# A linear-attention and gated feed-forward kernel: the cosine's table loaded by its own instruction, ten warm-ups instead of twelve, and the first block's sums with two slots per matmul

## The chip, the cores and the metric

The kernel runs on one core of one Trainium2 chip. The metric is the device time of one execution in microseconds; shorter is better. Several executions are timed and the median is given. One further execution is recorded by the hardware profiler, and every row quoted here comes from such a record.

## The reference

The reference has two parts. The first is a gated linear attention over `q`, `k`, `v` and `alpha`, each of 4 batches, 8 heads, 768 time steps and 48 features, all float32:

```python
for t in range(S):
    state = alpha[:, :, t, :, None] * state + einsum('bhd,bhe->bhde', k[:, :, t], v[:, :, t])
    y[:, :, t] = einsum('bhd,bhde->bhe', q[:, :, t], state)
```

Its output, laid out as 3072 tokens of 384 features, goes through a feed-forward layer with a hidden width of 2048:

```python
h = x @ w_in
g = h * np.cos(h)
return g @ w_out
```

The result is 3072 x 384 in float32.

## The kernel before

**Tiling.** Time is cut into 24 chunks of 128 steps (6 for each batch), and four chunks make a block (`R = 4`), so there are 6 blocks. Inside a chunk the recurrence is turned into matrix products: `alpha` goes through a logarithm, running sums of the logarithms are made by matmuls with triangular masks, their exponentials scale `q` and `k`, and then scores, masked scores, outputs and the chunk's state update are ordinary matmuls. The feed-forward layer works on pairs of chunks in four quarters of the hidden width: `ff1` fills a PSUM tile, `act` makes the cosine of it on ScalarE, `gate` multiplies the two on VectorE, and `ff2` accumulates the second product.

**Order.** Nothing is scheduled automatically. A long string, `ORDER`, names units one after the other, and every engine runs its share in that order. A word such as `w12` means `warmup(12)`; `ca1` means `cums0(1)`. The suffixes `:A`, `:D` and `:P` put a unit on ScalarE, VectorE or GpSimd. All loads and stores are issued by SyncE in the same order. The string begins

```python
"a1 la1 v1 a0 la0 k1 w12 ca1 xi1 xc1 ka1 w1 ca0 q1 qa1 xi0 ct0 xt0 xc0 k0 ka0 tk1 q0 w1 tq1 w2 kp0 v0 "
```

**The first block.** Blocks 0, 1 and 2 are halved by heads, so `n = 2 * block + half`. For block 0: `a1` loads half of `alpha` (four heads), `la1` (`ln0`, L267) takes its logarithm into `lna`, whose second index is the slot `i` of 4. `ca1` (`cums0`, L281) makes, for each slot, the sum over all four slots, each multiplied by the mask `t_incl` or `t_strict`: 16 matmuls of 192 columns. `xi1` and `xc1` (`exp0`, L310) are exponentials of that sum with both signs, `ka1` and `qa1` (`hat0`, L316) multiply them into `k` and `q`. `ca0` and its followers do the same for the other half. Then `tk` and `tq` (`pe_transposes`, L373) turn the results, `kp` and `kn` (`k_rows` and `ev_k_rows`) bring `k` back to rows of time, and `S`, `u`, `A`, `m`, `Y`, `y` are the state product, its update, the scores, the mask, the outputs and their copy. Blocks 1 and 2 are in `PFX`: GpSimd forms the running sum over the slots first (`pa`, L287), and `cums0` then needs only seven matmuls for a half.

**Warm-ups.** `warmup(n)` issues `n` matmuls of 512 columns on zeros into a PSUM bank that nobody reads (L520). Twelve of them stand ahead of `ca1` in TensorE's order, and single ones stand between later units.

**Tables.** `lnset` loads the table that holds logarithm and exponential by an instruction of its own when another table is in (L179). `act` only notes that its own table is in; the load of the cosine's table (the activation function is a sine with a bias of half pi) is put in by the compiler ahead of the first `activation` that needs it, and is then recorded under that line (L483). The program has twelve table loads: six of each kind.

**Feed-forward around a table load.** With `F` for `ff1` (L477), `f` for `act` (L483), `p` for `gate` (L489), `V` for `ff2` (L497), `Z` and `z` for loads of the two weights and `R...`, `r...` for their casts, a quarter is `F`, `f`, `p` and later two `V`. The six places where `f` follows a logarithm or an exponential on ScalarE are the six loads of the cosine's table.

Of the kernel before, what the change touches and what calls it, by code (L numbers as in the profile page):

```python
# [16 lines left out]
def kernel(  # L17
# [10 lines left out]
    nc = tc.nc  # L28
    B, H, S, D = q.shape
    DM, DF = moe_w_in.shape  # L30
    C = 128
# [4 lines left out]
    R = 4  # L36
    M = C // R
    HH = H // 2
# [6 lines left out]
    PFX = (1, 2,)  # L45
# [22 lines left out]
    lna = first[:, 0 : R * H * 64].rearrange("p (i h d) -> p i h d", i=R, h=H)  # L68
    nc.gpsimd.memset(lna[:, :, :, D:64], 0.0)

    sel_f, sel_bf, t_incl, t_strict = [], [], [], []
# [32 lines left out]
    w1 = consts.tile([C, 3, DF], BF, tag="w1")  # L104
    w2 = consts.tile([C, DF // C, DM], BF, tag="w2")
# [69 lines left out]
    table = [None]  # L175
# [81 lines left out]
    HW = HH * D  # L257
# [4 lines left out]
    def hs(n):  # L262
        return slice(HH * (n % 2), HH * (n % 2 + 1))
# [6 lines left out]
    def cums0(n):  # L270
        t = ps.tile([C, 2, 512], FP, tag="big", bufs=3)
        cum0[n] = t
        lay = min(n // 2, 1)
        for i in range(R):

            if n // 2 in PFX:
                terms = [(R - 1, t_incl[lay])] if i == R - 1 else [(R - 1, t_strict[lay]), (i, ident_bf)]
            else:
                terms = [(i2, t_incl[lay] if i2 <= i else t_strict[lay]) for i2 in range(R)]
            for x, (i2, mk) in enumerate(terms):  # L280
                nc.tensor.matmul(t[:, i // 2, HW * (i % 2) : HW * (i % 2 + 1)], mk, lna[:, i2, hs(n), 0:D],  # L281
                                 start=(x == 0), stop=(x == len(terms) - 1))


    def prefix0(n):
# [192 lines left out]
                                 start=(kk == 0), stop=(kk == 2))  # L478

    def act(g, qt):  # L480
        table[0] = "sin"
        c_sb = moe.tile([C, FQ, 2, C], BF, tag="c_sb", bufs=3)
        nc.scalar.activation(out=c_sb, in_=h_ps[g, qt], func=AF.Sin, bias=halfpi, scale=1.0)  # L483
        c_t[g, qt] = c_sb
# [30 lines left out]
    def warmup(n):  # L515
# [8 lines left out]
        "a": lambda j: load("a", alpha, j), "k": lambda j: load("k", k, j),  # L524
        "q": lambda j: load("q", q, j), "v": load_v, "vn": cast_v,
        "la": ln0, "ca": cums0, "pa": prefix0, "ct": totals0, "xt": exp_tot0,
        "xi": lambda n: exp0("i", n, -1.0), "xc": lambda n: exp0("c", n, 1.0),
        "ka": lambda n: hat0("k", KO, "i", n), "qa": lambda n: hat0("q", 0, "c", n),
# [14 lines left out]
        "D": x_transposes, "B": ev_x, "X": x_transposes_dma,  # L543
        "F": lambda n: ff1(n // 4, n % 4), "Fa": lambda n: ff1(n // 4, n % 4, slice(0, 1)), "Fb": lambda n: ff1(n // 4, n % 4, slice(1, 2)),
        "f": lambda n: act(n // 4, n % 4), "p": lambda n: gate(n // 4, n % 4),
        "V": lambda n: ff2(n // 4, n % 4), "e": ev_ff2, "o": store, "w": warmup,
    }

    ORDER = (
# [64 lines left out]
```

## Time and profile before

| | us |
|---|---|
| median of 3 timed runs | 186.07 |
| lowest and highest of them | 185.19, 187.74 |
| the profiled execution | 184.71 |
| its span in the profile | 182.9 |
| TensorE busy in it (matmuls) | 174.8 |
| VectorE, ScalarE, GpSimd busy | 137.8, 115.6, 88.7 |

The span runs from the first instruction of the program to its last; the profiled execution has 1.8 us outside it. Times inside the span are counted from its start. A row of the timeline gives the start, the duration, the engine, the line of the kernel, the operation and how many instructions of this kind followed each other; brackets give the idle time of the engine before the row and what ended it. Matmuls overlap each other, so the duration of one matmul is longer than the distance from its start to the next one's start; where a rate is wanted, that distance is taken.

### The profile page before, as it was taken

The page shows a single profiled execution, that of the slowest core. Times are in us where ns is not written, and L with a number is a line of the kernel's source. Part 1 is how long each engine was busy: PE and PEld are TensorE (multiplying, and loading weights), DVE is VectorE, ACT ScalarE, POOL GpSimd, SP SyncE. Part 2 cuts the span into 40 slices and gives each one's busy share as a digit, 9 for nine tenths or more (in the row PEclk, how much of TensorE's full clock was granted, in tenths as well). Part 3 has the DMA queues.
Part 4 walks back from the last instruction along what each step waited for, and adds up shares of the span by engine and source line. Part 5 has one row for each costly group of instructions (what it writes and reads, how often), then busy time and mean ns, then how long its engine had stood idle before and what let it go on. Part 6 is the DMA issues. An engine that isn't in the chain of part 4 may idle for free.

```text
span 182.9 us, 4471 instructions
## 1 busy us (share of the span) xinstructions
PE 174.8 (96%) x1828; PEld 128.3 (70%) x1828; DVE 137.8 (75%) x178; ACT 115.6 (63%) x154; POOL 88.7 (48%) x84
## 2 busy tenths in 40 slices
PE   7999879999999999999999999999999999999992
PEld 2765668867767777777767688677767876778750
DVE  7599787989856989789569896977867859447521
ACT  3599796586849888747969766455355365474330
POOL 8004936379294999999989965931010000000000
PEclk9999999999999999999999999999999999999999
DMA  5999999998999899999689799974988304111022
GB/s 144 327 306 353 379 350 372 319 261 215 289 255 274 239 264 266 274 292 274 155 233 240 206 215 275 204 178 130 170 200 221 86 0 134 28 59 46 0 86 86
DMA packets 71524, 38.43 MB, mean 210 GB/s; under 512 B 44112, under 2 KB 68432, under 8 KB 71504
## 3 DMA queue, kind: packets, MB, share of 16 engines
q1 hardware_dynamic: 71504, 38.15, 78.3%
q8 instruction: 14, 0.23, 0.5%
q14 instruction: 6, 0.05, 0.1%
HBM read 25.17 MB, written 4.72 MB: 163 GB/s over the span
## 4 chain that ended last, share of the span: by engine, by line
PE 80%; DMA 8%; DVE 5%; ACT 2%; SPq 2%; issue 1%; DVEq 0%; ACTq 0%
PE o_new L497 32%; PE t_new L477 27%; DMA t_new<-in_moe_w_out_dram 5%; PE w_new L520 4%; PE t L392 4%; PE t L281 3%; PE t_new L373 3%; PE t L437 2%; PE t L434 2%; PE t L413 2%; DMA t_new<-in_alpha_dram 2%; DVE t L398 1%; SPq L125 1%; DMA t_new<-pre 1%; DVE pre L316 1%
## 5 line engine op out<-in xcount | busy, mean ns | idle before, releaser
L497 PE MATMUL o_new<-w,g_new 128*128 128x384 bf16 x384 | 75.8, 326 | 0.8 <-ACT o_new L164 0.4
L483 ACT ACTIVATE c_sb<-t_new,halfpi 128x1024 bf16<-128x1024 f32 x48 | 53.2, 1113 | 31.6 <-PE t_new L477 29.6
L489 DVE TENSOR_TENSOR g_new<-t_new,c_sb 128x1024 bf16<-128x1024 f32 x48 | 57.8, 1218 | 19.1 <-ACT c_sb L483 19.0
L477 PE MATMUL t_new<-x_new,w 128*128 128x256 bf16 (+1 forms) x624 | 70.9, 264 | 1.3 <-DVE w L166 0.9
L477 PEld LDWEIGHTS <-w 128*128 128x128 bf16 x624 | 56.4, 98 | 11.1 <-DVE w L166 1.2
L497 PEld LDWEIGHTS <-g_new 128*128 128x128 bf16 x384 | 34.0, 97 | 18.7 <-DVE g_new L489 1.4
L398 DVE TENSOR_TENSOR t<-t,triu_f 128x1024 bf16<-128x1024 f32 x24 | 29.0, 1217 | 2.5 <-PE t L392 2.5
L164 ACT ACTIVATE o_new<-o_new 128x384 f32<-128x384 f32 x17 | 8.3, 487 | 10.6 <-PE o_new L497 10.6
L421 DVE TENSOR_TENSOR ub<-t,em 128x384 bf16<-128x384 f32 x20 | 11.1, 557 | 2.4 <-PE t L413 1.3
L166 POOL CAST vn<-t_new 128x384 bf16<-128x384 f32 x7 | 3.5, 505 | 19.3 <-DMA t_new<-in_v_dram 19.3
L166 POOL CAST w<-t_new 128x1536 bf16<-128x1536 f32 x6 | 8.8, 1466 | 7.5 <-DMA t_new<-in_moe_w_out_dram 5.2
L316 POOL TENSOR_TENSOR pre<-t_new 128x768 bf16<-128x768 f32 x5 | 9.9, 1977 | 4.0 <-DMA t_new<-in_alpha_dram 2.2
L164 ACT ACTIVATE y_new<-t 128x384 bf16<-128x384 f32 x16 | 7.8, 489 | 5.6 <-PE t L437 5.6
L437 PE MATMUL t<-vn,t 128*128 128x48 bf16 x192 | 11.3, 184 | 0.0
L520 PE MATMUL w_new<-lnb 128*128 128x512 bf16 x26 | 9.8, 497 | 1.2 <-DVE lnb L60 1.2
L244 POOL TENSOR_TENSOR pre<-t_new,icp 128x768 bf16<-128x768 f32 x6 | 10.9, 1816 | 0.2
L437 PEld LDWEIGHTS <-t 128*128 128x128 bf16 x192 | 9.7, 96 | 1.7 <-DVE ub L421 0.5
L244 POOL TENSOR_TENSOR pre<-t_new,cp 128x768 bf16<-128x768 f32 x6 | 10.9, 1814 | 0.1
L310 ACT ACTIVATE t_new<-t 128x768 f32<-128x768 f32 x12 | 9.3, 811 | 2.0 <-PE t L281 1.8
L420 DVE TENSOR_TENSOR t<-t,ub 128x384 f32<-128x384 f32 x16 | 8.9, 559 | 1.5 <-PE t L413 1.3
L287 POOL TENSOR_TENSOR first<-first 128x192 bf16<-128x192 bf16 x12 | 7.1, 596 | 5.8 <-ACT first L267 5.1
L483 ACT ACT_TABLE_LOAD x6 | 7.7, 1283 | 3.3 <-PE t_new L477 3.3
(79 smaller groups left out, 202.4 us busy)
## 6 DMA issues: line engine op xcount, KB each, us to landing
t_new<-in_v_dram SPq DMA_DIRECT2D x24, 192.0 KB, 4.0
out_dram<-o_new SPq DMA_DIRECT2D x11, 384.0 KB, 2.8
t_new<-in_alpha_dram SPq DMA_DIRECT2D x20, 192.0 KB, 4.0
t_new<-in_k_dram SPq DMA_DIRECT2D x20, 192.0 KB, 4.3
t_new<-in_q_dram SPq DMA_DIRECT2D x20, 192.0 KB, 3.9
t_new<-in_moe_w_in_dram SPq DMA_DIRECT2D x4, 768.0 KB, 9.2
t_new<-in_moe_w_out_dram SPq DMA_DIRECT2D x4, 768.0 KB, 9.7
t_new<-pre SPq DMA_DIRECT2D x12, 256.0 KB, 3.8
```

What stands on the lines that cost most here:

```text
L164: eng.activation(out=dst, in_=src, func=AF.Copy)
L166: eng.tensor_copy(out=dst, in_=src)
L244: el(nm, b).tensor_tensor(out=pre[:, b % 2, s, off : off + 64 * H].rearrange("p i (h d) -> p i h d", d=64)[:, :, :, 0:D], in0=blk_t[nm, b] ...
L316: pick(nc.vector).tensor_tensor(out=pre[:, b % 2, :, off + 64 * HH * (n % 2) : off + 64 * HH * (n % 2 + 1)].rearrange("p i (h d) -> p i h ...
L398: nc.vector.tensor_tensor(out=t.rearrange("s (h t) -> s h t", h=H), in0=A_ps.pop(j).rearrange("s (h t) -> s h t", h=H), in1=triu_f.unsquee ...
L421: nc.vector.tensor_tensor(out=ub[:, us(j)].rearrange("r p (a e) -> r p a e", a=2), in0=t.rearrange("r p (a e) -> r p a e", a=2), in1=em_t[ ...
L437: nc.tensor.matmul(t[:, h * D : (h + 1) * D], A_t[j][:, ACOL[h] * C : (ACOL[h] + 1) * C], vn_t[j][:, h], start=first, stop=True, skip_grou ...
L477: nc.tensor.matmul(t[:, f, js], w1[:, kk, ft * C : (ft + 1) * C], x_t[g][:, js, kk], start=(kk == 0), stop=(kk == 2))
L483: nc.scalar.activation(out=c_sb, in_=h_ps[g, qt], func=AF.Sin, bias=halfpi, scale=1.0)
L489: nc.vector.tensor_tensor(out=g_new, in0=h_ps.pop((g, qt)), in1=c_t.pop((g, qt)), op=ALU.mult)
L497: nc.tensor.matmul(o_ps[j][:, 0:DM], g[:, f, j % 2], w2[:, qt * FQ + f], start=(f == 0 and qt == 0), stop=(f == FQ - 1 and qt == 3))
L520: nc.tensor.matmul(w_t[0], warm[:, 0:C], warm, start=True, stop=True)
```

## The change

There are three edits, and nothing else is changed.

1. `act` issues the load of the cosine's table by an instruction of its own, just ahead of the activation in ScalarE's order, when another table is in. The number of table loads, and the place of each among ScalarE's instructions, stay the same; the semaphore wait that stood at the load, where there was one, now stands at the activation.
2. `w12` becomes `w10`.
3. In `cums0`, block 0 takes the slots two at a time: where two neighbouring slots of the result use the same mask for a given source slot, one matmul of 384 columns reads the source slot twice through a stride of zero and writes both. Where they need different masks, two matmuls of 192 columns remain. There are 10 matmuls for a half in place of 16, six of 384 columns and four of 192; the columns add up to 3072 as before. The source slot is now the outer loop.

```diff
         lay = min(n // 2, 1)
-        for i in range(R):
-
-            if n // 2 in PFX:
+
+        if n // 2 in PFX:
+            for i in range(R):
                 terms = [(R - 1, t_incl[lay])] if i == R - 1 else [(R - 1, t_strict[lay]), (i, ident_bf)]
-            else:
-                terms = [(i2, t_incl[lay] if i2 <= i else t_strict[lay]) for i2 in range(R)]
...
+            return
+
+        for i2 in range(R):
+            for a in range(2):
+                x = lna[:, i2, hs(n), 0:D]
+                if i2 in (2 * a, 2 * a + 1) and i2 % 2 == 1:
+                    for i, mk in ((2 * a, t_strict[lay]), (2 * a + 1, t_incl[lay])):
+                        nc.tensor.matmul(t[:, a, HW * (i % 2) : HW * (i % 2 + 1)], mk, x,
+                                         start=False, stop=(i2 == R - 1), skip_group_check=True)
+                else:
+                    nc.tensor.matmul(t[:, a, 0 : 2 * HW].rearrange("p (b f) -> p b f", b=2),
+                                     t_incl[lay] if i2 <= 2 * a else t_strict[lay],
+                                     lna[:, i2 : i2 + 1, hs(n), 0:D].rearrange("p o h d -> p o h d").to_broadcast([C, 2, HH, D]),
+                                     start=(i2 == 0), stop=(i2 == R - 1), skip_group_check=True)
...
     def act(g, qt):
-        table[0] = "sin"
+        if table[0] != "sin":
+            nc.scalar.preload_act_table_set("trig_and_small")
+            table[0] = "sin"
...
-        "a1 la1 v1 a0 la0 k1 w12 ca1 xi1 ...
+        "a1 la1 v1 a0 la0 k1 w10 ca1 xi1 ...
```

More of the change, by code (lines that the diff above doesn't have):

```diff
@@ L273, in cums0 @@
         lay = min(n // 2, 1)
-        for i in range(R):
-            if n // 2 in PFX:
+        if n // 2 in PFX:
+            for i in range(R):
                 terms = [(R - 1, t_incl[lay])] if i == R - 1 else [(R - 1, t_strict[lay]), (i, ident_bf)]
-            else:
-                terms = [(i2, t_incl[lay] if i2 <= i else t_strict[lay]) for i2 in range(R)]
-            for x, (i2, mk) in enumerate(terms):
-                nc.tensor.matmul(t[:, i // 2, HW * (i % 2) : HW * (i % 2 + 1)], mk, lna[:, i2, hs(n), 0:D],
-                                 start=(x == 0), stop=(x == len(terms) - 1))
+                for x, (i2, mk) in enumerate(terms):
+                    nc.tensor.matmul(t[:, i // 2, HW * (i % 2) : HW * (i % 2 + 1)], mk, lna[:, i2, hs(n), 0:D],
+                                     start=(x == 0), stop=(x == len(terms) - 1))
+            return
[11 more added lines that the diff above has]
+                                     start=(i2 == 0), stop=(i2 == R - 1), skip_group_check=True)
     def prefix0(n):
```

2 rows, old and new, of the table ORDER are left out of this document.

## The prediction

> **What bounds the kernel now.** I read the page first: busy times and slices, then the chain that ended last.
>
> ```profile
> PE 174.8 (96%) x1828; PEld 128.3 (70%) x1828; DVE 137.8 (75%) x178; ACT 115.6 (63%) x154; POOL 88.7 (48%) x84
> PE   7999879999999999999999999999999999999992
> DMA  5999999998999899999689799974988304111022
> PE 80%; DMA 8%; DVE 5%; ACT 2%; SPq 2%; issue 1%; DVEq 0%; ACTq 0%
> ```
>
> TensorE is busy 174.8 of 182.9 us and is 80% of the chain; the DMA engines are full over the first third. So a gain must either cut TensorE work at the start or close one of its gaps. The list of waits by engine says where these are:
>
> ```profile
> PE w_new L520 <- DVE lnb L60: 1.2, 1, 1.2
> PE t_new L477 <- DVE w L166: 0.9, 1, 0.9
> PE t L281 <- DVE t L398: 0.8, 1, 0.8
> PE t_new L477 <- DVE x_new L166: 0.5, 1, 0.5
> PE o_new L497 <- ACT o_new L164: 0.4, 1, 0.4
> PE o_new L497 <- DVE g_new L489: 0.3, 1, 0.3
> PE t_new L373 <- DVE pre L316: 0.2, 1, 0.2
> ```
>
> Seven waits (total, times, longest), 4.3 us with the 1.2 us before the first warm-up; another 3.6 us at the end follow the last matmul. The windows of the later stages show that after 60 us nothing is left to close (columns: stretch, length, then each engine's busy time):
>
> ```profile
> 50.00:60.00 10.00, 9.67 (x105) 7.24 (x101) 6.10 (x9) 7.24 (x10) 6.41 (x6) 1.00 0.95 265
> 60.00:80.00 20.00, 19.95 (x228) 15.32 (x227) 17.62 (x23) 14.58 (x21) 19.69 (x13) 1.00 0.94 266
> ```
>
> So what is gained before 60 us is kept if TensorE's work then simply starts sooner. The timeline of the stages that the change touches, TensorE and then ScalarE:
>
> ```profile
> 1.19 5.30 PE L520 MATMUL w_new<-lnb 128*128 128x512 bf16 x12 [1.19 <-DVE lnb L60]
> 6.28 1.69 PE L281 MATMUL t<-first 128*128 128x192 bf16 x16
> 7.81 0.38 PE L520 MATMUL w_new<-lnb 128*128 128x512 bf16 x1
> 8.03 1.48 PE L281 MATMUL t<-first 128*128 128x192 bf16 x16
> ```
>
> ```profile
> 4.40 0.84 ACT L267 ACTIVATE first<-t_new 128x768 bf16<-128x768 f32 x1 [2.38 <-DMA t_new<-in_alpha_dram]
> 6.46 0.84 ACT L267 ACTIVATE first<-t_new 128x768 bf16<-128x768 f32 x1 [1.21 <-DMA t_new<-in_alpha_dram]
> 8.01 2.35 ACT L310 ACTIVATE t_new<-t 128x768 f32<-128x768 f32 x3 [0.71 <-PE t L281]
> 54.70 1.28 ACT L483 ACT_TABLE_LOAD   x1 [2.18 <-PE t_new L477]
> 56.00 1.11 ACT L483 ACTIVATE c_sb<-t_new,halfpi 128x1024 bf16<-128x1024 f32 x1
> 69.25 1.28 ACT L483 ACT_TABLE_LOAD   x1 [1.07 <-PE t_new L477]
> ```
>
> The logarithm that `ca1` needs ends at 4.40 + 0.84 = 5.24, but TensorE reaches `ca1` only at 6.28, behind the twelve warm-ups; ScalarE waits for it until 8.01. Two of the six loads of the cosine's table wait for a matmul before they begin.
>
> **The change part by part: ten warm-ups.** The last warm-ups start 0.427 us apart, a 512-column matmul later 0.216 us apart (7.81 to 8.03): TensorE is at half speed here, though the page's clock row shows nothing of it. The trace's clock record begins at 6.70, inside `ca1`: its first two matmuls start 0.160 us apart, the later ones 0.0825. Two warm-ups less put `ca1` at 6.28 - 0.853 = 5.43, 0.19 after its logarithm. But if the clock still rises at 6.70, 1.27 us of `ca1` now run at half speed instead of 0.42: 8 of its 16 pieces of 192 columns take 1.27, the other 8 take 0.66, and it hands over at 7.36 instead of 7.81. I take 0.45 us, not 0.85. The bounds are 0.85 (the clock rises after `ca1`) and a loss, which is the first rival.
>
> The Trainium skill, page "TensorE: Matmul & The Clock Gate", section "What's actually happening", has the full clock granted after a busy window of about 3.4 us whose phase is free of the program. By it the rise at 6.70 would stay where it is when two warm-ups go, as I assume; but in other executions it would lie elsewhere, and the gain would vary, by my estimate from that page, between about 0.2 and 0.85.
>
> **Two slots per matmul.** 32 matmuls become 20, with the same 6144 columns. The nearest row of 384 columns is `ff2`'s L497: four in 0.65 us, 0.1625 each, against 2 x 0.0825 = 0.165 for two of 192. Twelve pairs give 0.03 us. Twelve weight loads go too, but they lie beside matmuls (L281's loads take 0.098 each on PEld, with no gap between the matmuls). No row shows a moving operand with a stride of zero. Lower bound of its price: nothing. Upper bound: the source counts twice, 0.1625 more for each of twelve, 1.95 us. I take nothing, since L281 already reads 48 of every 64 elements at the rate of the contiguous L497 (0.43 and 0.42 ns a column). The new order of the terms costs nothing: the exponential reads all four slots at once.
>
> **The table.** The same twelve loads of 1.283 us remain. Where the load already follows its predecessor at once (23.40, 87.69, 98.11, 105.94) nothing changes. The one at 54.70 can start at 52.52, when ScalarE became free, and is over at 53.80, before its matmuls end at 54.6; the cosine starts at 54.7 instead of 56.0, its gate at 55.9 instead of 57.15. TensorE waited for that gate only the 0.33 us of the list (58.10 to 58.43), so of 1.3 us on ScalarE 0.33 counts. If GpSimd, busy 19.69 of the 20 us that follow, is late next with the scaled `q` and `k` of blocks 2 and 3, even that goes: bounds 0 and 0.33. The load at 69.25 starts 1.07 earlier, in a stretch in which TensorE idles 0.05: I count 0.
>
> The Trainium skill, page "ScalarE: Activation LUTs", section "What ACT_TABLE_LOAD costs", adds some 1.38 us of draining to the 1.283. The rows do not show it: the cosine follows the load by 1.30 us. By the page the gain at 54.70 would be up to 2.18 us on ScalarE, and on TensorE still 0.33.
>
> **Does the 0.45 arrive?** Following it: the exponentials start at 7.56 (their engine is free at 7.30), VectorE's first product at 8.40 instead of 8.85 (its `k` landed at 7.61). The fourth product needs the `q` that landed at 11.28, so it moves only from 11.52 to 11.30. VectorE's next gap, 0.195 us at 14.68 behind the first state product, gives most of that back: that product comes 0.45 sooner, VectorE 0.41. From there to 21.0 VectorE has no gap over 0.04, so `ca3`, which waits for its mask, moves by 0.4. The next TensorE waits (26.75, 30.98, 39.56) hang on VectorE and ScalarE work of the same chain. DMAs do not move: the eight 768 KB weight loads land 2.0 to 2.9 us apart with the engines full, the last at 34.60, then `k` until 36.88 and `q` until 39.68. Their casts and products on GpSimd stay where they are; the last of them, 39.84 to 42.46, is read by TensorE at 43.2, so 0.7 us of room is left. SyncE's order is unchanged and no DMA is added.
>
> **Sum against the profiled execution:** 184.71 - 0.40 - 0.33 = about 184.0. That execution lies 1.36 us under the median of the timed runs; the same 0.7 us off the median gives 185.4.
>
> **The rivals.** *The clock rises a window later (slower).* `ca1` now follows the warm-ups with 0.19 us to spare. If `alpha` lands more than that later than 4.38, TensorE has a hole just before the clock would rise. From the first warm-up to the rise it took 5.51 us of unbroken work; if a hole starts that anew at 5.43, the rise comes at 10.9. Then `ca1` takes 16 x 0.160 = 2.56 and ends at 8.0, one warm-up goes to 8.4, `ca0` takes 2.56 and ends at 11.0 instead of 9.35: 1.6 us late, 1.4 after the slack of VectorE's queue, less 0.33 from the table: 187.1. Against it: in this trace there is no hole, and any hole would be a few tenths. *The zero stride halves the rate (slower).* 1.95 - 0.45 - 0.33: +1.2 us, 187.2; against it speaks only the pitch of the old reads. *The start is hidden.* The full DMA engines and GpSimd behind them hold the time at 44 us; only the table's 0.33 or less remains: 185.9. For it: GpSimd waits for a landing at 25.00, 27.91, 30.35, 34.65, 37.09 and 39.84. Against it: TensorE waited for none of these. *The load does not move:* the changed program's listing has it without a wait and the wait at the cosine, so this gets no chance of its own. *Far faster:* all seven waits and the two warm-ups together are 5.2 us, but no edit reaches more than a part of them.
>
> **How the numbers follow.** Forecast (0.3 to 1.3 us faster) 0.56; the start hidden 0.22; the clock 0.11; the stride 0.06; something larger on the fast side that no row shows 0.05. The three timed runs lie 2.55 us apart, so 2% (3.7 us) is about what a measurement of this kernel can tell from no change; no case by itself leaves that band, and I give the outside 0.06 on each side, for the slower cases on top of scatter and for what I cannot see. The range holds the forecast's own 184.7 to 185.8, the hidden start, most of the two slower cases (187.2) and half the runs' scatter: 183.8 to 187.3.
>
> **What would show it right or wrong.** In the profile after: `ca1` should start near 5.4, with ten matmuls that hand over near 7.4; the exponentials at about 7.6; the pace of the 384-column matmuls should be 0.16 us once the clock is up and twice 0.16 before. The second load of the cosine's table should follow its predecessor at once and the cosine its matmuls. TensorE's wait for `g_new` (0.3) should be gone from the list, and the waits at 21.0, 26.75 and 30.98 should be as long as before but 0.4 earlier. The forecast is wrong if these waits grow by what the start gained, if the clock record begins near 10, or if `ca1` at full clock takes over 2 us.

## The result and the profile after

The changed kernel takes 184.41 us, the median of 20 runs (183.6 to 186.05); the kernel before took 186.24 in its 20 runs beside them (184.62 to 187.74). The ratio is 0.9926, with a 95% interval of 0.9898 to 0.9954: faster, clear of noise, by 0.5 to 1.0%. The ratio leaves out executions more than 1.5% above the fastest of their kernel, so where a kernel scatters more than that, the medians of all its runs are given beside it.

The profiled execution took 184.25 us with a span of 182.5, 0.46 less than the one before (184.71). TensorE's work is 0.9 us less:

```profile
PE 173.9 (95%) x1814; PEld 127.0 (70%) x1814; DVE 137.2 (75%) x178; ACT 115.8 (63%) x154; POOL 89.4 (49%) x84
PE 71%; SPq 9%; DVE 9%; DMA 5%; issue 3%; ACT 2%; DVEq 0%
```

The start, TensorE's timeline (start, duration, line, shape, count, wait before):

```profile
1.19 4.45 PE L534 MATMUL w_new<-lnb 128*128 128x512 bf16 x10 [1.19 <-DVE lnb L60]
5.43 0.58 PE L291 MATMUL t<-first 128*128 128x384 bf16 x2
...
6.01 0.81 PE L291 MATMUL t<-first 128*128 128x384 bf16 x4
6.66 0.33 PE L288 MATMUL t<-first 128*128 128x192 bf16 x2
6.82 0.38 PE L534 MATMUL w_new<-lnb 128*128 128x512 bf16 x1
7.38 0.48 PE L291 MATMUL t<-first 128*128 128x384 bf16 x2 [0.18 <-ACT first L267]
```

`ca1` starts at 5.43 as forecast, with 2 + 4 matmuls of 384 columns. It is over at 6.8 and not at 7.36: the trace's clock record begins at 5.60 here, where it was 6.70 before. TensorE now waits for the second logarithm (7.38). What VectorE makes of it, in the changed kernel:

```profile
8.06 1.88 DVE L328 TENSOR_TENSOR pre<-t_new 128x768 bf16<-128x768 f32 x2 [2.81 <-ACT t_new L322]
10.17 0.96 DVE L328 TENSOR_TENSOR pre<-t_new 128x768 bf16<-128x768 f32 x1 [0.23 <-DMA t_new<-in_k_dram]
11.43 0.96 DVE L328 TENSOR_TENSOR pre<-t_new 128x768 bf16<-128x768 f32 x1 [0.30 <-DMA t_new<-in_q_dram]
```

The first product starts 0.79 us sooner (8.85 before), the fourth only 0.09 (11.52 before), because `q0` lands at 11.34. ScalarE around the two table loads that had waited:

```profile
52.39 1.28 ACT L494 ACT_TABLE_LOAD   x1
54.58 1.11 ACT L497 ACTIVATE c_sb<-t_new,halfpi 128x1024 bf16<-128x1024 f32 x1 [0.90 <-PE t_new L489]
...
67.74 1.28 ACT L494 ACT_TABLE_LOAD   x1
69.03 1.11 ACT L497 ACTIVATE c_sb<-t_new,halfpi 128x1024 bf16<-128x1024 f32 x1
```

Both follow their predecessors at once, and the cosine at 54.58 now waits for its matmuls instead of its table. TensorE at the gate that hangs on this cosine, first before, then after:

```profile
56.62 1.47 PE L477 MATMUL t_new<-x_new,w 128*128 128x256 bf16 x12
58.43 0.82 PE L497 MATMUL o_new<-w,g_new 128*128 128x384 bf16 x4 [0.33 <-DVE g_new L489]
```

```profile
56.48 1.47 PE L489 MATMUL t_new<-x_new,w 128*128 128x256 bf16 x12
57.79 0.81 PE L511 MATMUL o_new<-w,g_new 128*128 128x384 bf16 x4
60.46 0.82 PE L511 MATMUL o_new<-w,g_new 128*128 128x384 bf16 x4 [0.21 <-DVE g_new L503]
```

The first wait is gone. From start to start the second row now comes 1.31 us after the first, where it was 1.81: the wait held TensorE up by 0.50 us, though its bracket says 0.33, since the bracket counts from the end of the last matmul, and matmuls overlap. A new wait of 0.21 us stands before the next gate. VectorE around the gate that hangs on it, first before, then after (the first row of each is the gate `p8`, the third is `ka5`, the fourth the gates `p9` and `p10`):

```profile
57.15 1.22 DVE L489 TENSOR_TENSOR g_new<-t_new,c_sb 128x1024 bf16<-128x1024 f32 x1 [1.56 <-ACT c_sb L483]
58.29 0.55 DVE L166 CAST y_new<-t 128x384 bf16<-128x384 f32 x1
58.75 0.97 DVE L316 TENSOR_TENSOR pre<-t_new 128x768 bf16<-128x768 f32 x1
59.65 2.34 DVE L489 TENSOR_TENSOR g_new<-t_new,c_sb 128x1024 bf16<-128x1024 f32 x2
```

```profile
55.72 1.22 DVE L503 TENSOR_TENSOR g_new<-t_new,c_sb 128x1024 bf16<-128x1024 f32 x1 [0.28 <-ACT c_sb L497]
56.86 0.55 DVE L166 CAST y_new<-t 128x384 bf16<-128x384 f32 x1
57.33 1.94 DVE L328 TENSOR_TENSOR pre<-t_new 128x768 bf16<-128x768 f32 x1
59.19 2.34 DVE L503 TENSOR_TENSOR g_new<-t_new,c_sb 128x1024 bf16<-128x1024 f32 x2
```

The first gate comes 1.43 us sooner, but the second pair only 0.46, since `ka5` took 1.94 in place of 0.97.

**A ruler for the stages.** The 384 matmuls of `ff2` come in the same order in every kernel here. The starts of numbers 16, 32, 64 and 80 (counted from 0) cut the span into five stages. In us, from the trace of each profiled execution, the kernels being those of the experiments below. "Clock rises" is where the trace's clock record begins; from there on the same matmuls start about twice as close together (the warm-ups of `q_early_warm12`, 0.43 and then 0.22 us apart around 3.99):

| kernel | clock rises | to 16 | 16 to 32 | 32 to 64 | 64 to 80 | 80 to end |
|---|---|---|---|---|---|---|
| before | 6.70 | 39.56 | 4.81 | 14.06 | 7.36 | 117.13 |
| changed | 5.60 | 39.27 | 4.96 | 13.56 | 7.54 | 117.14 |
| one_warm10 | 4.65 | 39.69 | 6.30 | 14.05 | 8.79 | 117.13 |
| one_table | 5.41 | 39.71 | 5.03 | 13.56 | 7.93 | 117.13 |
| one_slots | 5.94 | 39.42 | 5.17 | 14.19 | 7.91 | 117.13 |
| two_not_warm | 5.78 | 39.33 | 6.57 | 13.56 | 7.51 | 117.14 |
| before_apart | 6.38 | 39.40 | 5.13 | 14.05 | 7.98 | 117.11 |
| after_apart | 4.88 | 39.60 | 5.03 | 13.57 | 7.00 | 117.14 |
| before_apart_table | 7.08 | 39.74 | 4.90 | 13.56 | 7.00 | 117.21 |
| after_apart_no_table | 4.18 | 39.11 | 5.10 | 14.06 | 7.84 | 117.39 |
| before_apart2 | 5.21 | 40.18 | 6.29 | 14.05 | 7.45 | 117.13 |
| after_apart2 | 5.34 | 39.20 | 5.15 | 13.56 | 7.93 | 117.34 |

From 80 on all are within 0.3 us, so everything is decided before number 80 starts, at 65 to 69 us. Between the two profiled executions: -0.29, +0.15, -0.50, +0.18, 0.01, together -0.45.

### The profile page after: what moved, and what is told of

Read it like the earlier page. It is cut to its first block, busy times and chain, and to the rows that moved or that the text cites. A ratio compares the mean times of both kernels' runs of the same rounds, so it can differ in the third digit from the quotient of the medians.

```text
span 182.5 us, 4443 instructions
## 1 busy us (share of the span) xinstructions
PE 173.9 (95%) x1814; PEld 127.0 (70%) x1814; DVE 137.2 (75%) x178; ACT 115.8 (63%) x154; POOL 89.4 (49%) x84
## 4 chain that ended last, share of the span: by engine, by line
PE 71%; SPq 9%; DVE 9%; DMA 5%; issue 3%; ACT 2%; DVEq 0%
PE o_new L511 30%; PE t_new L489 30%; SPq L125 5%; DMA t_new<-in_q_dram 4%; PE t L404 3%; DVE pre L328 2%; PE t L449 2%; PE t L425 2%; SPq L120 2%; DMA t_new<-in_alpha_dram 2%; PE t L446 2%; DVE t L410 1%; SPq L135 1%; PE t_new L385 1%; DVE w L166 1%
## 5 line engine op out<-in xcount | busy, mean ns | idle before, releaser
L328 DVE TENSOR_TENSOR pre<-t_new 128x768 bf16<-128x768 f32 x7 | 7.8, 1118 | 3.3 <-ACT t_new L322 2.8
L534 PE MATMUL w_new<-lnb 128*128 128x512 bf16 x24 | 9.0, 484 | 1.2 <-DVE lnb L60 1.2
```

The source lines that it names most:

```text
L328: pick(nc.vector).tensor_tensor(out=pre[:, b % 2, :, off + 64 * HH * (n % 2) : off + 64 * HH * (n % 2 + 1)].rearrange("p i (h d) -> p i h ...
```

## The experiments

### Each edit alone

`one_warm10` is the kernel before with

```diff
- "a1 la1 v1 a0 la0 k1 w12 ca1 ...
+ "a1 la1 v1 a0 la0 k1 w10 ca1 ...
```

> The kernel before with ten warm-ups for twelve and nothing else. Theory A (the terms of the prediction): the first block's sum starts 0.85 us sooner, runs longer at half clock, hands over up to 0.45 us sooner and less where the second logarithm (end at 7.30) is the later of the two; 0.3 to 0.4 us of that reach the end: ratio 0.998. Theory B (the warm-ups carry the measured 0.74%, since VectorE, ScalarE and TensorE all start sooner): ratio 0.993 to 0.995. Theory C (the start is hidden by the full DMA engines): 1.000.

Measured: 186.52 us median (12 runs, 185.28 to 187.84) beside 186.34 for the kernel before (35 runs); ratio 1.0038 (0.9996 to 1.0081). Theory B falls, and A's 0.3 to 0.4 us are not there either. Its profile has the two logarithms at

```profile
4.42 0.84 ACT L267 ACTIVATE first<-t_new 128x768 bf16<-128x768 f32 x1 [2.40 <-DMA t_new<-in_alpha_dram]
6.91 0.84 ACT L267 ACTIVATE first<-t_new 128x768 bf16<-128x768 f32 x1 [1.65 <-DMA t_new<-in_alpha_dram]
```

The second half of `alpha` landed at 6.88 and `q0` at 11.76, and TensorE stood 0.79 us before `ca0`. Set against the landing of `q0`, the start of `ff2` number 16 lies 27.92 to 27.96 us later in nine of the twelve profiles of the table, with ten warm-ups or twelve. It lies 28.17 to 28.28 later in three: before, `before_apart` and `before_apart_table`. These have twelve warm-ups and a clock that rises at 6.38 or later. So with a rise up to 5.94 two warm-ups are worth nothing in this stage. No profile has ten warm-ups and a late rise, so whether ten would have saved the 0.24 to 0.35 us is not shown.

`one_table` is the kernel before with

```diff
-        table[0] = "sin"
+        if table[0] != "sin":
+            nc.scalar.preload_act_table_set("trig_and_small")
+            table[0] = "sin"
```

> The kernel before with the cosine's table loaded by an instruction of its own and nothing else. Theory A: TensorE's wait of 0.33 us for the gate near 58.4 goes, nothing else: ratio 0.998. Theory B (warm-ups carry it): 0.999 to 1.000, the wait moves to the next place. Theory D (the table carries it: in the timed runs more of TensorE's waits than in the profiled one hang on the two loads that wait, 1.28 and 1.07 us on ScalarE): 0.993 to 0.995.

Measured: 185.22 (12 runs, 184.05 to 187.24), ratio 0.9955 (0.9909 to 1.0001). This lies on theory D's side of A, but the interval reaches from D to 1. By the medians it is 1.12 us less. In its profile the first gate's wait is gone, but TensorE waits 0.59 us for the next gate.

`one_slots` has the new `cums0` only.

> The kernel before with two slots per matmul in the first block's sums and nothing else. Theory A: 0.03 us of TensorE time, ratio 1.000. Theory E (fewer weight loads matter while the clock is at half, where each load takes 0.15 us): up to 0.2 us, 0.999. The distance from one 384-column matmul to the next at full clock should be 0.1625 us; 0.32 would mean that a stride of zero halves the rate.

Measured: 186.29 (12 runs), ratio 1.001 (0.9968 to 1.0052): no change that shows. In the changed kernel's trace the 384-column matmuls start 0.1625 us apart (6.009, 6.171, 6.334), the rate of contiguous operands: a stride of zero costs nothing.

`two_not_warm` is the changed kernel with `w12`.

> The changed kernel with twelve warm-ups again (table and slots changed). Theory A: the table's 0.33 us and the slots' 0.03 stay, ratio 0.998. Theory B: 0.999 to 1.000. Theory D: 0.993 to 0.995. If the three single edits add up to less than the whole change, the rest is an interplay of the start with the table.

Measured: 185.97 (12 runs, 184.17 to 187.34), ratio 0.9934 (0.9891 to 0.9978): D's figure, though its median is only 0.37 under that of the kernel before, which is theory A's 0.998. By the ratios, table and slots without the warm-ups hold what the whole change shows. By the medians they do not: 185.97 lies 1.56 above the changed kernel, and one run of twelve is under 184.7 us, where the changed kernel has 15 of 20. The next sections bear on this.

### What makes the scatter

Two of these four profiles have a wait of 1.6 us near 45 that neither kernel had in its own. GpSimd and then VectorE in `one_warm10`, and the same in the kernel before:

```profile
39.71 1.82 POOL L316 TENSOR_TENSOR pre<-t_new 128x768 bf16<-128x768 f32 x1 [0.76 <-DMA t_new<-in_q_dram]
39.96 2.38 DVE L316 TENSOR_TENSOR pre<-t_new 128x768 bf16<-128x768 f32 x1
45.53 0.62 PE L373 MATMUL t_new<-ident_bf,pre 128*128 128x128 bf16 x8 [1.62 <-DVE pre L316]
```

```profile
39.84 2.62 POOL L316 TENSOR_TENSOR pre<-t_new 128x768 bf16<-128x768 f32 x1 [0.73 <-DMA t_new<-in_q_dram]
39.83 0.95 DVE L316 TENSOR_TENSOR pre<-t_new 128x768 bf16<-128x768 f32 x1
43.91 0.62 PE L373 MATMUL t_new<-ident_bf,pre 128*128 128x128 bf16 x8 [0.25 <-DVE pre L316]
```

VectorE's `ka2` and GpSimd's `qa3` come due at the same moment. In the kernel before VectorE was first by 0.01 us, and GpSimd's product took 2.62 in place of 1.82. In `one_warm10` GpSimd was first, and VectorE's product took 2.38 in place of 0.95, ending 0.8 us after GpSimd's. TensorE's wait is for the next product in VectorE's queue, `qa2`, which starts that much later; in `one_warm10` and before:

```profile
44.46 1.02 DVE L316 TENSOR_TENSOR pre<-t_new 128x768 bf16<-128x768 f32 x1
```

```profile
42.90 0.96 DVE L316 TENSOR_TENSOR pre<-t_new 128x768 bf16<-128x768 f32 x1
```

The Trainium skill, page "SBUF — State Buffer", section "Who interferes with whom", says that an instruction of VectorE with two inputs in SBUF contends with a GpSimd instruction that reads SBUF, that the port pair they share is an exclusive lock, and that the order of issue decides who blocks. The traces agree, and have a figure for it. In all fourteen profiles, `ka2` or `ka5` that starts while a product of GpSimd runs (`pre` or `pp`) ends 0.81 or 0.82 us after that product, whenever it started. A GpSimd product of this size that starts while one of these two runs ends 1.66 to 1.68 us after it (1.79 where the two overlap by 0.03 only). So the later one does nearly all its work after the other's end: 0.81 of 0.95 us, or 1.67 of 1.82.

`before_apart` moves one word, so that `ka2` starts a gate earlier:

```diff
- "p4 p5 ka2 V2 p6 ...
+ "p4 ka2 p5 V2 p6 ...
```

> The kernel before with one word of the order moved: block 1's first scaled k on VectorE (ka2) ahead of the gate p5 instead of behind it, so that it starts near 38.7 and no longer at the same moment (39.6 to 40.0) as GpSimd's scaled q (qa3). Theory F (chance order of the two decides: where GpSimd starts first, VectorE's product takes 2.4 to 2.6 us instead of 0.95 and TensorE waits 1.6 us near 45): the product is 0.95 to 1.2 in the profile, TensorE's wait near 44 is under 0.5, and the median falls by 0.4 to 1.0 us, ratio 0.995 to 0.998. Theory G (the collision costs, but TensorE makes it good later): ratio 1.000.

Measured: 185.46 (12 runs); ten of the twelve lie between 184.98 and 185.59, where the kernel before beside it ran from 184.31 to 188.52 (35 runs, median 186.52). The ratio is 1.0003 (0.9964 to 1.0042); by the medians it is 1.06 us less. By the ratio this is theory G, by the medians theory F; the two part here for the reason given with the result. The product took 1.28 and TensorE's wait was 0.57, both a little over F's bounds. Both ends of the scatter went, not the upper one alone.

`after_apart` is the changed kernel with the same move.

> The changed kernel with the same move of ka2. Theory F: its runs that lie 1.3 us above the others go, median down by 0.2 to 0.5 us against the changed kernel, ratio to before 0.989 to 0.992; against the kernel before with the same move, what is left is the table, 0.3 to 0.6 us. Theory H (the change is faster because its VectorE wins the start at 39.6 more often): against the kernel before with the same move nothing is left, under 0.2 us. Theory G: as the changed kernel, 0.993.

Measured: 184.26 (12 runs, 183.83 to 186.06), ratio 0.9952 (0.9912 to 0.9993). F expected 0.2 to 0.5 us against the changed kernel; there were 0.15, and four runs still lay above 185.2. Against `before_apart` 1.20 us are left. So H falls for the larger part: of the 1.83 us between the medians of the two kernels, 1.20 do not live on who wins at 39.6, and that is twice to four times the table's 0.3 to 0.6.

`before_apart2` also puts `ka5` behind `p9`:

```diff
- ... v9 o1 V20 ka5 p9 em2 ...
+ ... v9 o1 V20 p9 ka5 em2 ...
```

> The kernel before with ka2 moved and also block 2's scaled k (ka5) behind the gate p9 instead of ahead of it, so that a long collision of ka5 with GpSimd (1.7 to 2.4 us instead of 0.95 near 57 to 60) no longer holds up the gate that TensorE waits for. Theory D (the table's gain in the timed runs comes from that gate, which hangs on the cosine behind the load): the waits of TensorE between 57 and 65 sum to under 0.5 us, and this kernel gains another 0.3 to 1.0 us over the one with ka2 alone moved. Against it: no further change.

> The changed kernel with both moves. Theory D: with the gate no longer held up, the table's gain is only the 0.33 us of the prediction, so this kernel is 0.2 to 0.4 us faster than the kernel before with both moves, and the fastest of the four; ratio to before 0.985 to 0.991. If the table's gain has nothing to do with the collisions, the distance to the kernel before with both moves stays at 0.8 us or more.

Measured: 185.47 (ratio 1.0002, 0.9966 to 1.0037) and 184.81 (0.996, 0.9921 to 0.9998). The first does not gain over `before_apart`, against theory D; in its profile `q0` came late (12.22) and the earlier `ka2` met another GpSimd product (2.44 us). The second is not the fastest of the four. The distance between the two is 0.66 us, between the two expectations. Moving `ka5` is no improvement, and these two alone do not say why the table is worth 1.2.

### The table by itself, with the collision out of the way

`before_apart_table` is `before_apart` with the table edit; `after_apart_no_table` is `after_apart` without it, which leaves ten warm-ups and the slots.

> The kernel before with ka2 moved ahead of p5 and the table loaded by its own instruction. Theory T (the table alone makes the 1.2 us between the two kernels with ka2 moved): median 184.2 to 184.6 where the kernel before with ka2 moved had 185.46; from the first matmul of the second output product of pair 0 to the first of pair 2 (ff2 number 32 to 64) 13.56 us instead of 14.05. Theory W (the start is worth a part): 184.8 or more.

> The changed kernel with ka2 moved and the table left to the compiler: ten warm-ups and two slots per matmul only. Theory T: as the kernel before with ka2 moved, 185.3 to 185.6. Theory W: 185.0 or less.

Measured: 184.26 (6 runs, 183.83 to 185.11), ratio 0.9884 (0.9834 to 0.9934), and 185.63 (12 runs, 184.73 to 187.61), ratio 0.9992 (0.9953 to 1.0031). Theory T holds both ways (185.63 is 0.03 above its range). With the table: 184.26 whether the other edits are there or not. Without it: 185.46 and 185.63. The two of each pair were timed at different times, beside runs of the kernel before of 186.52 and 186.19. The stage 32 to 64 is 13.56 or 13.57 with the edit in all six profiles that have it and 14.05 to 14.19 in the six others. Where the rest sits is seen in `before_apart`, TensorE's waits and VectorE's rows behind the gate:

```profile
58.58 0.82 PE L497 MATMUL o_new<-w,g_new 128*128 128x384 bf16 x4 [0.33 <-DVE g_new L489]
61.68 0.82 PE L497 MATMUL o_new<-w,g_new 128*128 128x384 bf16 x4 [0.63 <-DVE g_new L489]
```

```profile
57.30 1.22 DVE L489 TENSOR_TENSOR g_new<-t_new,c_sb 128x1024 bf16<-128x1024 f32 x1 [1.56 <-ACT c_sb L483]
58.44 0.55 DVE L166 CAST y_new<-t 128x384 bf16<-128x384 f32 x1
58.91 1.58 DVE L316 TENSOR_TENSOR pre<-t_new 128x768 bf16<-128x768 f32 x1
60.42 2.34 DVE L489 TENSOR_TENSOR g_new<-t_new,c_sb 128x1024 bf16<-128x1024 f32 x2
```

and in `before_apart_table`, which has neither wait (TensorE is busy 10.00 us of 55 to 65, against 9.04):

```profile
56.14 1.22 DVE L491 TENSOR_TENSOR g_new<-t_new,c_sb 128x1024 bf16<-128x1024 f32 x1 [0.28 <-ACT c_sb L485]
57.28 0.55 DVE L166 CAST y_new<-t 128x384 bf16<-128x384 f32 x1
57.74 1.38 DVE L316 TENSOR_TENSOR pre<-t_new 128x768 bf16<-128x768 f32 x1
59.04 2.34 DVE L491 TENSOR_TENSOR g_new<-t_new,c_sb 128x1024 bf16<-128x1024 f32 x2
```

The whole queue of VectorE behind the gate moves by 1.2 to 1.4 us, so here TensorE's second wait goes too. Stages 32 to 80 take 22.03 and 20.56 us: 1.47 less.

The second wait does not go in every execution with the edit: it is 0.21 in the changed kernel's profile, 0.17 in `two_not_warm` and 0.59 in `one_table`. What decides is `ka5`, which ends 0.81 us after the GpSimd product beside it and so takes 0.97 to 2.39 us. Set against its duration, the stage 64 to 80 of the ten profiles with `ka5` in its old place reads:

| | duration of `ka5`, us | stage 64 to 80, us |
|---|---|---|
| without the edit | 0.97, 1.46, 1.58, 1.66, 2.39 | 7.36, 7.84, 7.98, 7.91, 8.79 |
| with the edit | 1.02, 1.38, 1.90, 1.94, 2.32 | 7.00, 7.00, 7.51, 7.54, 7.93 |

Without the edit, what `ka5` takes longer the stage takes longer, nearly one for one. With it, `ka5` is free up to about 1.4 us. At equal `ka5` the edit is worth, by an estimate from these rows, 0.4 to 0.8 us in this stage beside the 0.50 of the stage before: 0.9 to 1.3 together, and the medians say 1.20 and 1.37. The pair of profiles at the start had 0.97 before and 1.94 after, and so hid it.

### The start with `q0` earlier

`q_early_warm10` and `q_early_warm12` are `after_apart` with `v1` issued behind `q0`, and with ten and twelve warm-ups.

> The changed kernel with ka2 moved and the load of v's first chunk (v1) moved behind q0 in SyncE's order. Theory Q (what the warm-ups give is hidden by the landing of q0, behind which VectorE's fourth product starts 0.09 us later): q0 lands near 10.5 instead of 11.3, the fourth product no longer waits for it, and the first 384-column ff2 after the e1 copy (ff2 number 16) lies 0.3 to 0.7 us ahead of 39.2 to 39.6. The time itself falls less, since GpSimd and the k and q of block 1 wait for the full DMA engines until 39.7: 183.8 to 184.3. Rival: the DMA queue is the bound as a whole, nothing moves.

> The same with twelve warm-ups. Theory Q: with q0 out of the way the two warm-ups show: ff2 number 16 lies 0.3 to 0.45 us behind that of the ten (at the same moment of the clock's rise), the time 0.1 to 0.4 us more. Rival: no difference, since the second logarithm or another landing is the bound.

Measured: 186.35 (12 runs, ratio 1.0027, 0.9996 to 1.0057) and 186.79 (12 runs, 1.0061, 1.0018 to 1.0104). Both are slower than `after_apart`, by 2.1 and 2.5 us. `a0` landed sooner (5.43 and 5.45, was 6.78), but `q0` at 11.32 and 12.07, within the 11.19 to 12.22 of the other twelve profiles. With little gained there, a wait of TensorE of 1.2 to 1.4 us near 18 opened, behind a logarithm of ScalarE that waited 1.57 and 1.36 us for a later piece of `alpha`, and `ff2` number 16 came at 42.03 and 41.39. This is nearer the rival: the engines were full, and a load moved ahead only changed which one was late. As a test of the warm-ups it failed, for the two landed `q0` at different times.

A second thing happened in `q_early_warm10`. Behind waits of 0.55 and 1.41 us its clock record falls to half from 18.34 to 21.76, and 192-column matmuls there start 0.16 us apart instead of 0.08. Its `ff2` number 16 comes 30.71 us after `q0`, against 29.32 in `q_early_warm12`, which has waits of 1.23 and 1.21 us and no such stretch, and 27.93 in `after_apart`. So the lost clock cost it about 1.4 us, as far as two executions can be compared. By the mean clock of each run, 14 of the 24 runs of these two kernels lost about this much or more (0.980 to 0.991). Of the runs of the kernel before beside the experiments, 99, two did (0.987 and 0.989), and none of any other kernel here (0.996 or more).

## Why the prediction was right, and where it was not

**The verdict.** Faster was forecast, with 185.4 and a range of 183.8 to 187.3; 184.41 lies inside. For the profiled execution it said about 184.0, and it was 184.25. But the sum was near in part by luck: two of its terms were wrong, in opposite directions.

**The warm-ups: the step that failed.** The working had 0.45 us at the hand-over of `ca1` and 0.40 at the end, from "if the clock still rises at 6.70". It rose anywhere from 3.99 to 7.08 in the fourteen profiles, so the profiled 6.70 was a late one. And behind `ca1` the fourth product waits for `q0`, which the working named but let through by a gap at 14.68. The profiled start did come 0.29 us sooner (the waits of 21.0, 26.75 and 30.98 are at 20.71, 26.45 and 30.69, as long as before), and the next stage gave 0.15 of it back. But `two_not_warm`, with twelve warm-ups and a rise at 5.78, reached the same stage only 0.06 us later with `q0` landing 0.06 later. The single edit is 1.0038 (0.9996 to 1.0081). And with the meeting of `ka2` and `qa3` out of the way, twelve warm-ups (`before_apart_table`) and ten (`after_apart`) both have 184.26. In effect this term belonged to the rival of the hidden start, with another landing than the ones named there. What stays open is the 1.56 us between the medians of the changed kernel and `two_not_warm`, which differ by the two warm-ups alone: they may shift who wins that meeting, but no run shows it, and the two were not timed side by side.

**The table: the right mechanism, mis-sized.** The load moved as forecast, and the 0.33 us wait behind the first gate went: 0.50 us in that stage, every time, for the wait's bracket left out what the overlap of matmuls hides. The term left out what stands behind the gate on VectorE: a copy, `ka5`, and `p9`, for which TensorE waits next. In the profiled execution `ka5` took 0.97 and there was no second wait, so nothing was to be seen. In the other four profiles without the edit and with the old place of `ka5` it took longer beside GpSimd, and the stage 64 to 80 was 7.84 to 8.79 and not 7.36. The table alone is worth 1.20 us by the medians of `before_apart` and `before_apart_table`. GpSimd takes part of the gain back, but by another way than the late product that the prediction named: by what it makes of `ka5`. The sign "TensorE's wait for `g_new` should be gone" failed on this, with 0.21 us left.

**The slots.** Forecast 0.03 us and no price for the zero stride; the pace is the forecast 0.1625 and the time unchanged.

**The other rivals.** The clock a window later: TensorE had holes of 0.79 us or more ahead of `ca0` in `one_warm10`, `after_apart` and `before_apart2`, but after the clock had risen, and there the clock stayed. No profile had a hole ahead of the rise, so what one would cost there stays open; a clock lost later is seen in `q_early_warm10` alone. The Trainium skill, page "TensorE: Matmul & The Clock Gate", section "What's actually happening", has the window free-running, so that the place of the rise is a matter of phase; that it moved by 3.1 us between executions agrees. The section's spread of 500 ns either way does not.

**What no step had.** The start of `ka2` and `qa3` within 0.01 us of each other stood in the profile before and was read past. It moves TensorE's wait by about 1.4 us from one execution to the next. That most of the scatter of the kernel before comes from it is likely, since ten of the twelve runs of `before_apart` lie within 0.61 us. The medians lie 1.8 us apart and the table accounts for about 1.2. The remaining 0.6 is a place where the changed kernel may win that meeting more often; `before_apart` and `after_apart` show that it could be worth that, but how often each side wins was not counted, and it stays open.

No version clearly beat the changed kernel: `after_apart` and `before_apart_table` have 184.26, 0.15 us less, well inside their scatter.

## What to carry to other kernels

Price a moved wait by all that stands behind it in its consumer's queue, and not only by the first idle time it causes: the second wait may be hidden in the one execution that was profiled. Where two engines start work on the same memory within some hundredths of a microsecond of each other, the profile shows one outcome of two; move one of them before anything else is judged. A filler ahead of a stage is only worth removing when its end, and no landing further on, is what the stage's last consumer waits for.

## What the runs showed of the hardware

The clock's rise lies anywhere from 2.8 to 5.9 us after the first matmul at 1.19 (3.99 to 7.08 in the span), with ten or twelve unbroken warm-ups from there. Two products on VectorE and GpSimd that start together cost the later one 0.8 us (GpSimd: 1.82 to 2.62) or 1.4 to 1.65 us (VectorE: 0.95 to between 2.38 and 2.60); the later one ends 0.81 us (VectorE) or 1.67 us (GpSimd) after the earlier one. In one profile the clock was lost for 3.4 us behind waits of 0.55 and 1.41 us within ten microseconds. A matmul whose moving operand repeats through a stride of zero runs at the full 0.1625 us for 384 columns.
